# Gate-loop attention and SwiGLU feed-forward on one core: weights pieces no longer wait for rotated rows, and weights weigh half as much in the list schedule

## The chip, the cores and the metric

The kernel runs on one core of a Trainium2 chip. The metric is the device time of one execution in microseconds (us): the median of three runs, lower is better. The profile is a separate execution of the same program; times inside it count from the start of its span.

## The reference, cut to what matters

The first half is a linear attention with complex gates, the second a feed-forward network on its output.

```python
# 4 batches x 8 heads, 768 steps, head width 48
mag = np.sqrt(a_re * a_re + a_im * a_im)
scale = np.minimum(mag, 0.999) / (mag + 1e-06)
ar, ai = a_re * scale, a_im * scale                  # a complex gate for each step and feature
for t in range(S):
    new_re = ar[t] * S_re - ai[t] * S_im             # the state is turned and shrunk by the gate
    new_im = ar[t] * S_im + ai[t] * S_re
    S_re, S_im = new_re + outer(k[t], v[t]), new_im
    y[t] = q[t] @ S_re
# x: (3072 tokens, 384 features), w_gate and w_val: (384, 1536), w_out: (1536, 384)
xn = x / np.sqrt(np.mean(x * x, -1) + 1e-06) * rms_g
out = (silu(xn @ w_gate) * (xn @ w_val)) @ w_out
```

The three weight matrices come as 64-bit floats, so the kernel narrows them itself.

## The kernel before, in words

**Chunks, units, groups.** The 24 chunks n of 128 tokens are handled one after another. Gates are prepared by units u: unit 0 is chunk 0, unit 1 is chunk 1, and from unit 2 on a unit is two chunks. The feed-forward runs by groups g of two chunks.

**Gates of a unit** (`gates(u)`). ScalarE and VectorE compute the size of the gates (squares, reciprocal roots, a running product by scans), then their angle (Arctan, running sum by scans, then Abs and two Sin), and VectorE multiplies q and k with cosine and sine into a tile `rot`. Six DMAs issued by SyncE (`kq<-rot`, line 1123) then carry the rotated rows of a chunk from `rot` into the layout `kq` that the attention reads; their landing is what the attention waits for. `kq` and `rot` exist twice, for even and odd chunks.

**Attention of a chunk** (`attend(n)`). TensorE computes scores (`bank<-kq`, two halves in two PSUM banks), VectorE copies them under the causal mask into `am` (two copies), TensorE computes y (`bank<-am,ve` and `bank<-kq,state`), transposes k (`bank<-ident,kq`, evacuated by ScalarE as `kt`) and updates the state (`bank<-vn,kt`; VectorE adds and decays it as `state`). Then the norm: ScalarE squares y (`sq`), TensorE sums it (`bank<-ones,sq`), VectorE makes `ssv` of it, GpSimd its power of -1/2 (`rs`), TensorE spreads that over the partitions (`bank<-ident,rs`), and VectorE writes the normed rows `xT`.

**Feed-forward of a group** (`feed(g, xT)`). Six blocks b; each is six matmuls with `wg` into one bank and six with `wv` into another (the trace shows two passes for each, so x12), ScalarE takes Silu of the first (`sg`), VectorE the product (`hT`). The product with `wo` follows in parts of four matmuls (x8), some of which stand between the blocks.

**Weights.** Twelve pieces: pieces 0 to 5 are `wg` and `wv` in thirds (even pieces `wg`, odd `wv`, 1.5 MB each), pieces 6 to 11 are sixths of `w_out` (768 KB each). GpSimd issues the DMA of a piece (`fetch`) into a place inside `wo` or `hT` that an earlier piece has left, and a copy of one element into `junk`, which waits for the landing. A piece also waits until the piece two before it has landed. Narrowing a piece (`narrow`) is one conversion on ScalarE and three operations on VectorE: a shift (`TENSOR_SCALAR`), a mask (`SCALAR_TENSOR_TENSOR`) and an addition (`CUSTOM_DVE_ANT_0` in the trace). Piece 4 has one more wait: `CLEAR = {4: 1}` lets it wait for `cleared[1]`, a one-column copy by GpSimd (`seen<-kq`) that itself waits for the rotated rows of chunk 1. The same copy is made for chunk 0.

**What sets the order.** Nothing is ordered by hand. Every operation is recorded with an estimated duration and its dependences (`add`). `dates` gives it a due time, back from its users, and shifts that by the entry of its stage in the table `flow.shift`; stages are for example ("w", 4), ("kq", 2), ("attend", 1). `schedule` then walks through time, takes on each free engine the ready operation with the earliest due time, and models the transfers: each issuing queue has its first DMA in flight, and the flying ones share the DMA engines in proportion to their `packet`. The order that results is fixed in the program: at run time every engine works strictly through its list. Where the scheduler expects TensorE to stand still before 62 us, it puts in idle matmuls (`bank<-rot`, "fillers") that keep TensorE's clock up. All operations are issued from line 676, so the profile is read by tiles.

Of the kernel before, what the change touches and what calls it, by code (L numbers as in the profile page):

```python
# [461 lines left out]
class Flow:  # L462
# [9 lines left out]
    turn = 0.0  # L472
# [50 lines left out]
    def add(self, eng, calls, dur, reads=(), writes=(), table=None, land=None, due=None, after=(), behind=(), late=None, mode=None, group=None):  # L523
        op = dict(i=len(self.ops), eng=eng, calls=calls, dur=dur, deps=set(), table=table, land=land,
                  base=due, late=late, mode=mode, group=group, stage=self.stage, behind={o["i"] for o in behind})
        self.ops.append(op)
        op["deps"].update(o["i"] for o in after)
        for ap in reads:
            self.note(op, ap, False)
        for ap in writes:  # L530
            self.note(op, ap, True)
        return op
# [146 lines left out]
def fast(tc, ctx, qT, kT, v, a_re, a_im, w_gate, w_val, w_out, rms_g, out, H, bad):  # L679
# [107 lines left out]
    def run(x):  # L787
        n = 1
        for step, size in reversed([tuple(y) for y in x.ap][0 if x.tensor.name in outside else 1:]):
            if step != n:  # L790
                break
            n *= size
        return n

    def dma(o, x, eng="SP", slow=0.0, **kw):
        n = mybir.dt.size(o.dtype)
        for s in o.shape:
            n *= s
        row = mybir.dt.size(o.dtype) * min(run(o), run(x))
        load = n / row * (0.006 + 50.3e-6 * row) / 16  # L800
        op = add(eng, [(QUEUE[eng].dma_start, (), dict(out=o, in_=x))], 0.85 if eng == "POOL" else 0.62, [x], [o],
                 land=2.0 + 1.4 * load + slow, **kw)
        op["slow"] = slow
        op["load"] = load
        op["packet"] = max(0.07, 0.006 + 50.3e-6 * row * (2 if eng == "POOL" and row == 2048 else 1))
        return op

    def mms(list_, dur, **kw):
# [53 lines left out]
    row = room("row", [P, C])  # L862
# [31 lines left out]
    for o, order in ((band, "p (x h) -> p x h"), (head, "p (x h) -> p h x")):  # L894
        add("DVE", [(nc.vector.tensor_reduce, (), dict(out=o, in_=ident.rearrange(order, h=H), axis=mybir.AxisListType.X,
                                                       op=ALU.add))], 0.3, [ident], [o], late=LATE)
# [22 lines left out]
    AHEAD = 2  # L919
    landed = {}  # L920

    CLEAR = {4: 1}

    def fetch(i, piece, raw, eng):
        to, ap, c, f = piece
# [7 lines left out]
        else:  # L933
            wait = []
        if eng == "POOL" and i in CLEAR:
            wait = wait + [cleared[CLEAR[i]]]
        sent = dma(raw3, src, eng, after=wait)
# [48 lines left out]
    turn = {}  # L986
# [59 lines left out]
    def gates(u):  # L1046
        ns = UNITS[u]
        nt = len(ns)
        T = nt * C
        t = loaded.pop(u) if u in loaded else load_kq(u, load_gates(u))  # L1050
        flow.stage = "size", u
        re, im, q, k = (t[x] for x in ("re", "im", "q", "k"))
        t1, t2, t3, t4, t5 = (t[f"t{i}"] for i in range(1, 6))
        act(t1, re, AF.Square)
        act(t2, im, AF.Square)
        if u in SUMMED:
            sums = []
            for i in range(nt):
                cs = slice(i * C, (i + 1) * C)
                ps = bank()[:, 0:ND * C].rearrange("p (j t) -> p j t", j=ND)  # L1060
                mms([(ps, ident, x[:, :, cs], a == 0, a == 1) for a, x in enumerate((t1, t2))],
                    2 * mm_time(ND * C))
                sums.append(ps)
                act(t2[:, :, cs], ps, AF.Abs_reciprocal_sqrt)
        else:
            tt(t1, t1, t2, ALU.add)
            act(t2, t1, AF.Abs_reciprocal_sqrt)
        act(t2, t2, AF.Square, scale=-EPS_MAG, bias=ones)
        act(t3, re, AF.Abs_reciprocal_sqrt, due=-200.0 if u == 0 else None)
        act(t3, t3, AF.Square, due=-200.0 if u == 0 else None)  # L1070
        if u in SUMMED:
            for i in range(nt):
                cs = slice(i * C, (i + 1) * C)
                ts(t1[:, :, cs], sums[i], CAP * CAP, None, ALU.min)
        else:
            ts(t1, t1, CAP * CAP, None, ALU.min)
        for j in range(ND):
            for i in range(nt):
                cs = slice(i * C, (i + 1) * C)
                scan(t4[:, j, cs], t2[:, j, cs], t1[:, j, cs], 1.0, ALU.mult, ALU.mult)  # L1080

        tt(t["f"], t["in"], t3.unsqueeze(1).to_broadcast([P, 2, ND, T]))
        stt(im, t5, 2.0, t3, ALU.subtract, rev=True)
        act(re, re, AF.Abs, bias=mid)
        act(re, re, AF.Relu, bias=width, accum=range_[:, u:u + 1])

        flow.stage = "root", u
        root = act(t2, t4, AF.Abs_reciprocal_sqrt)
        act(t1, t2, AF.Square)
        stt(t1, t1, -0.5, t4, ALU.mult)  # L1090
        stt(t2, t1, 1.5, t2, ALU.add)
        tt(q, q, t4)

        roots.append(root)
        yield
        flow.stage = "turn", u
        act(im, im, AF.Arctan, after=roots[-2:])
        last = turn.get(u - 1) if ns[0] % NCH else None
        for j in range(ND):
            scan(t3[:, j], im[:, j], zeros[:, 0:T], last[:, j] if last is not None else 0.0,  # L1100
                 ALU.add, ALU.add)
        n = t5.bitcast(I32)
        act(n, t3, AF.Copy, scale=0.5 / PI)
        stt(im, n, -2 * PI, t3, ALU.mult, ALU.add)
        turn[u] = im[:, :, T - 1:T]
        act(t5, im, AF.Abs)
        act(t3, im, AF.Sin)
        act(t5, t5, AF.Sin, scale=-1.0, bias=halfpi)

        for i, n_ in enumerate(ns):  # L1110
            e = slice(i * C + C - 1, i * C + C)
            tt(ends[:, :, n_:n_ + 1], t4[:, :, e], t2[:, :, e])
        flow.stage = "rot", u
        tt(t["f"], t["f"], t2.unsqueeze(1).to_broadcast([P, 2, ND, T]))
        for i, n_ in enumerate(ns):
            cs = slice(i * C, (i + 1) * C)
            for a, f in enumerate((t5, t3)):
                x = tt(rots[n_ % 2][:, a * ND:(a + 1) * ND].rearrange("p j (o t) -> p j o t", t=C), t["kq"][:, :, :, cs],
                   f[:, :, cs].unsqueeze(2).to_broadcast([P, ND, 2, C]))
                if not started:  # L1120
                    started.append(x)
        for n_ in ns:
            moved[n_] = [dma(kqs[n_ % 2][r:D2:2 * ND], rots[n_ % 2][:, r], "SP") for r in range(2 * ND)]
            if n_ < 2:
                cleared[n_] = copy(seen, kqs[n_ % 2][:, 0, 0:1], eng="POOL")
                cleared[n_]["dur"] = 1.2
        send_decays(u)
# [5 lines left out]
    def bank():  # L1133
        i = bank_turn[0]
        bank_turn[0] = (i + 1) % 4
        return banks[i]
# [231 lines left out]
    for in_, limit, op in ((ef, P_MIN, ALU.is_ge), (ef, 1.0, ALU.is_le), (range_, 0.0, ALU.is_le),  # L1368
# [15 lines left out]
    flow.warm = dict(after=started, until=WARM, call=[  # L1384
        (nc.tensor.matmul, (banks[3][:, 0:C],), dict(lhsT=filler[:, 0:C], rhs=filler[:, C:2 * C], start=True, stop=True))])
    flow.shift = {
        ("attend", 0): -38.4, ("attend", 1): -1.9, ("attend", 2): -16.2, ("attend", 3): -0.7,
        ("attend", 4): -35.7, ("attend", 6): -12.2, ("attend", 11): -3.9, ("attend", 18): 6.0,
        ("attend", 19): -5.7, ("attend", 20): -1.5, ("attend", 21): 11.1, ("attend", 22): 4.2, ("feed", 4): 7.5,
        ("feed", 7): 1.6, ("feed", 8): 4.4, ("feed", 9): 16.9, ("feed", 11): -26.3, ("kq", 2): -10.9,  # L1390
        ("kq", 6): -3.3, ("kq", 7): -15.8, ("kq", 9): 8.6, ("load", 1): -4.5, ("load", 2): -33.3,
        ("load", 3): 50.7, ("load", 11): -5.2, ("load", 12): -6.8, ("norm", 0): -0.8, ("norm", 1): -5.1,
        ("norm", 5): -4.6, ("norm", 16): 4.4, ("norm", 20): 1.8, ("norm", 21): -20.2, ("norm", 22): -8.0,
        ("root", 1): -1.3, ("root", 2): -5.7, ("root", 3): 41.8, ("root", 5): 2.8, ("root", 9): 9.4,
        ("rot", 1): -4.3, ("rot", 2): 0.4, ("rot", 3): -2.6, ("rot", 5): 10.3, ("rot", 10): -10.2,
        ("rot", 12): 4.7, ("size", 2): -2.7, ("size", 3): 14.9, ("size", 7): -0.3, ("size", 10): 14.6,
        ("size", 11): 53.4, ("size", 12): 18.6, ("state", 0): 20.7, ("state", 1): -6.7, ("state", 2): -18.1,
        ("state", 3): -5.4, ("state", 4): -2.1, ("state", 10): 0.2, ("state", 14): -4.9, ("state", 20): -17.7,
        ("turn", 0): -5.1, ("turn", 1): -18.8, ("turn", 4): 7.1, ("turn", 5): 47.3, ("turn", 6): -2.5,
        ("turn", 8): -28.6, ("turn", 9): 0.3, ("turn", 11): -2.5, ("w", 0): -2.6, ("w", 3): -20.3, ("w", 5): -3.8,  # L1400
        ("w", 6): -7.5, ("w", 10): -31.1, ("y", 0): -12.7, ("y", 1): -1.0, ("y", 7): 1.7, ("y", 10): 4.5,
        ("y", 11): -0.4, ("y", 15): 0.8, ("y", 17): -2.8, ("y", 20): 2.2,
    }
    flow.schedule()
    with tc.manual_schedule():
# [51 lines left out]
```

## Time and profile before

| | us |
|---|---|
| median of 3 runs (lowest, highest) | 721.65 (721.41, 721.87) |
| the profiled execution, whole | 723.45 |
| its span, first to last instruction | 721.7 |
| TensorE busy | 685.9 (95%) |
| VectorE busy | 476.2 (66%) |
| ScalarE busy | 328.6 (46%) |
| GpSimd busy | 65.5 (9%) |
| mean granted TensorE clock | 0.991 |

The span is 1.75 us shorter than the profiled execution's own time and equal to the median of the runs to 0.05 us. A share of busy time is an average: here the stretch up to about 118 us, where the gates of the first chunks, the weights and the first group meet, is very different from the 600 us that follow.

### The profile page before, as it was taken

What the parts mean: (1) busy time and instruction counts of PE and PEld (TensorE: products, weight loads), DVE (VectorE), ACT (ScalarE), POOL (GpSimd) and SP (SyncE); (2) the same over time, 40 slices, a digit from 0 to 9 for tenths busy, and PEclk for the clock granted to TensorE, in tenths of its full rate; (3) what the DMA queues carried; (4) which work ended last, traced back from release to release, by engine and by line L of the source; (5) the groups of instructions that cost most, each with busy time, mean ns of one, the idle gap of its engine ahead of it and who ended that gap; (6) DMA issues with size and microseconds to landing.
All of it is one profiled execution on the core that took longest, in us unless ns stands there. A gap on an engine that the chain in (4) does not pass through costs nothing.

```text
span 721.7 us, 16275 instructions
## 1 busy us (share of the span) xinstructions
PE 685.9 (95%) x6910; PEld 602.1 (83%) x6910; DVE 476.2 (66%) x756; ACT 328.6 (46%) x448; POOL 65.5 (9%) x106
## 2 busy tenths in 40 slices
PE   0779999999999999999999999999999999999996
PEld 0768877886889889889889889889889889989886
DVE  8998879878788778768757677777553432224121
ACT  8657648866677663837324743735510110010010
POOL 3232100010100001110001001010010000000000
PEclk9988999999999999999999999999999999999999
DMA  9897555535566355463554445444132410020000
GB/s 305 257 279 218 167 147 142 139 97 129 172 151 150 63 131 137 117 173 75 162 111 116 134 106 154 123 90 96 29 75 41 107 7 5 22 56 2 23 1 27
DMA packets 104000, 81.83 MB, mean 113 GB/s; under 512 B 41936, under 2 KB 94416, under 8 KB 103920
## 3 DMA queue, kind: packets, MB, share of 16 engines
q1 hardware_dynamic: 98560, 64.78, 32.8%
q0 software_dynamic: 4416, 15.35, 9.4%
q8 instruction: 56, 0.92, 0.6%
q10 hardware_dynamic: 944, 0.59, 0.3%
q14 instruction: 24, 0.20, 0.1%
HBM read 55.84 MB, written 4.72 MB: 84 GB/s over the span
## 4 chain that ended last, share of the span: by engine, by line
PE 86%; DMA 4%; DVE 4%; ACT 3%; SPq 1%; issue 1%; POOL 0%; DVEq 0%; ACTq 0%; POOLq 0%
PE bank L676 86%; DMA wo<-in_w_val_dram 2%; DMA wo<-in_w_gate_dram 1%; SPq L676 1%; DVE turns L676 1%; ACT turns L676 1%; ACT t L676 1%; ACT L676 1%; DMA in<-in_a_re_dram 1%; DVE rot L676 1%; DVE wv L676 1%; DMA decay<-ends 0%; DVE hT L676 0%; ACT wo L676 0%; POOL rs L676 0%
## 5 line engine op out<-in xcount | busy, mean ns | idle before, releaser
L676 PE MATMUL bank<-xT,wg 128*128 128x256 f32 x864 | 203.5, 386 | 0.0
L676 PE MATMUL bank<-xT,wv 128*128 128x256 f32 x864 | 201.4, 383 | 0.0
L676 PEld LDWEIGHTS bank<-xT,wg 128*128 128x128 f32 x864 | 162.7, 192 | 23.7 <-issue 2.0
L676 PEld LDWEIGHTS bank<-xT,wv 128*128 128x128 f32 x864 | 161.2, 190 | 22.2 <-issue 0.8
L676 ACT ACTIVATE sg<-bank 128x512 f32<-128x512 f32 x72 | 43.0, 597 | 171.1 <-PE bank L676 170.8
L676 DVE TENSOR_TENSOR hT<-bank,sg 128x512 f32<-128x512 f32 x72 | 49.6, 689 | 104.6 <-PE bank L676 99.1
L676 PE MATMUL bank<-wo,hT 128*128 128x192 f32 (+1 forms) x576 | 117.2, 356 | 0.6 <-DVE hT L676 0.5
L676 PEld LDWEIGHTS bank<-wo,hT 128*128 128x128 f32 x576 | 96.0, 190 | 12.3 <-DVE hT L676 1.0
L676 ACT ACT_TABLE_LOAD x64 | 82.1, 1283 | 17.7 <-DVE rot L676 10.2
L676 POOL TENSOR_TENSOR rs<-ssv,mhalf 128x1 f32<-128x1 f32 x24 | 24.8, 1034 | 501.2 <-DVE ssv L676 455.2
L676 DVE TENSOR_TENSOR rot<-kin,turns 128x768 f32<-128x768 f32 x48 | 44.1, 952 | 5.1 <-DMA kq<-rot 4.8
L676 ACT ACTIVATE kt<-bank 128x384 f32<-128x384 f32 x40 | 19.4, 488 | 57.8 <-PE bank L676 55.9
L676 PE MATMUL bank<-sums,hT 128*128 128x192 f32 x240 | 44.3, 327 | 0.0
L676 DVE COPY_PREDICATED am<-causal,bank 128x512 f32<-128x512 int32 x48 | 33.6, 725 | 15.3 <-PE bank L676 15.2
L676 PEld LDWEIGHTS bank<-sums,hT 128*128 128x128 f32 x240 | 39.8, 190 | 0.2
L676 DVE TENSOR_TENSOR hT<-hT 128x768 f32<-128x768 f32 x40 | 38.2, 956 | 0.7
L676 PEld LDWEIGHTS bank<-kq 96*32 96x32 f32 x1536 | 31.0, 112 | 8.8 <-issue 7.6
L676 PE MATMUL bank<-am,ve 128*32 128x128 f32 x768 | 37.3, 275 | 0.0
L676 PE MATMUL bank<-kq 96*32 96x128 f32 (+3 forms) x1536 | 35.4, 240 | 1.1 <-DMA kq<-rot 1.1
L676 ACT ACTIVATE t<-t 128x768 f32<-128x768 f32 (+1 forms) x39 | 30.7, 789 | 8.7 <-DVE t L676 8.3
L676 ACT ACTIVATE turns<-in 128x768 f32<-128x768 f32 (+1 forms) x39 | 30.1, 790 | 8.1 <-DVE in L676 6.1
L676 PE MATMUL bank<-kq,state 96*32 96x128 f32 x640 | 32.5, 272 | 0.2 <-DVE state L676 0.2
(123 smaller groups left out, 727.7 us busy)
## 6 DMA issues: line engine op xcount, KB each, us to landing
kq<-rot SPq DMA_DIRECT2D x144, 128.0 KB, 3.1
kin<-in_q_dram SPq DMA_DIRECT2D x24, 192.0 KB, 3.4
kin<-in_k_dram SPq DMA_DIRECT2D x24, 192.0 KB, 3.5
wo<-in_w_gate_dram SPq DMA_DIRECT2D x6, 768.0 KB, 5.9
wo<-in_w_val_dram SPq DMA_DIRECT2D x6, 768.0 KB, 5.7
wo<-in_w_out_dram SPq DMA_DIRECT2D x6, 768.0 KB, 4.6
out_dram<-ot SPq DMA_DIRECT2D x23, 192.0 KB, 2.3
in<-in_a_re_dram SPq DMA_DIRECT2D x11, 384.0 KB, 4.3
```

Source lines behind the costliest of these rows:

```text
L676: fn(*args, **kw)
```

## The change

Four things change in the code. Piece 4 no longer waits for chunk 1's rotated rows (`CLEAR` is empty). The two GpSimd copies `seen<-kq` are not made. In the scheduler's model of transfers, a piece of weights with rows over 2048 bytes has its `load` times 0.78 and its `packet` times 0.5. And the table of shifts is another one: many entries are changed and some are new.

```diff
-        load = n / row * (0.006 + 50.3e-6 * row) / 16
+        piece = eng == "POOL" and row > 2048
+        load = n / row * (0.006 + 50.3e-6 * row) / 16 * (0.78 if piece else 1.0)
...
-        op["packet"] = max(0.07, 0.006 + 50.3e-6 * row * (2 if eng == "POOL" and row == 2048 else 1))
+        op["packet"] = max(0.07, 0.006 + 50.3e-6 * row * (0.5 if piece else 1.0))
...
-    CLEAR = {4: 1}
+    CLEAR = {}
...
-            if n_ < 2:
+            if n_ in CLEAR.values():
                 cleared[n_] = copy(seen, kqs[n_ % 2][:, 0, 0:1], eng="POOL")
                 cleared[n_]["dur"] = 1.2
...
     flow.shift = {
-        ("attend", 0): -38.4, ("attend", 1): -1.9, ("attend", 2): -16.2, ("attend", 3): -0.7,
...
+        ("attend", 0): -38.4, ("attend", 1): -1.9, ("attend", 2): -4.4, ("attend", 3): -1.4, ("attend", 4): -35.7,
...
+        ("load", 0): 14.7, ("load", 1): -4.5, ("load", 2): -50.1, ("load", 3): 105.5, ("load", 5): 38.7,
...
+        ("turn", 12): -31.4, ("w", 0): -3.6, ("w", 1): -1.4, ("w", 2): -15.6, ("w", 3): -22.6, ("w", 4): -1.7,
...
```

The arithmetic is the same; what the program gets is another order on each engine. Up to the second group the orders of the two built programs differ in these places:

- GpSimd: the two `seen` copies are gone; `rs` of chunk 0 now stands before the `junk` copy that waits for piece 5, then come that copy and the DMA of piece 4, then the DMA of piece 7, then `rs` of chunk 1.
- ScalarE: of the first angles, the conversion of piece 1 no longer stands between the rounding copy and Abs of unit 0. Later, the conversion of piece 5 comes after the squares and roots of unit 2 instead of before them, still ahead of `sq` of chunk 1. In group 0 the operations on `in` with `mid` and `width` and the first square of unit 3 come after the Silu of block 2, ahead of unit 2's Arctan.
- VectorE: the masked copies `am` of chunk 0 come before the addition of piece 1 and before all operations on piece 0. The addition for piece 5 and the first sum of unit 2 come after `xT` of chunk 1 instead of before it. Piece 4's three operations come after the scans of unit 2 and after the first `hT`.
- TensorE: 33 fillers before the first group's matmuls instead of 46; 16 instead of 33 before the scores of chunk 0. The first half of chunk 1's scores stands before chunk 0's state update, the second half after it. Chunk 1's state update stands before the first group's matmuls instead of between blocks 4 and 5. Before the scores of chunk 2 there is one part of the product with `wo` instead of two.
- SyncE: the first look at `w_gate` (a second load of the weights, `wo<-in_w_gate_dram`, used by a range test) stood between the rotated rows of chunks 2 and 3 and now comes after the six `decay` loads and the values of chunk 5; the q and k loads of unit 3 now precede the six `decay` loads.

## The prediction

> **What bounds the kernel now.** I read the page first, for shares and slices, then the chain of waits in order of time, then the timelines of the engines up to 120 us.
>
> ```profile
> span 721.7 us, 16275 instructions
> ...
> PE 685.9 (95%) x6910; PEld 602.1 (83%) x6910; DVE 476.2 (66%) x756; ACT 328.6 (46%) x448; POOL 65.5 (9%) x106
> ...
> PE   0779999999999999999999999999999999999996
> ...
> PEclk9988999999999999999999999999999999999999
> ```
>
> TensorE is busy in all slices but the first three and the last. Of its 35.8 us of idle time, 19.8 lie before its first instruction and 6.1 after its last. The chain of waits says the same: from 108.85 us it is matmuls.
>
> ```profile
> 90.65 9.07 DMA wo<-in_w_gate_dram
> ...
> 102.52 3.37 DMA decay<-ends
> ...
> 108.85 444.69 PE bank L676 x4007
> ```
>
> So the order after that is worth little (its gaps sum to 0.75 us), and the change is priced by when TensorE gets through the start. Three marks carry it: F, the first matmul of group 0; K, the scores of chunk 2; G, the first matmul of group 1. TensorE's timeline:
>
> ```profile
> 55.81 4.89 PE L676 MATMUL bank<-xT,wg 128*128 128x256 f32 x12
> 60.54 2.75 PE L676 MATMUL bank<-xT,wv 128*128 128x256 f32 x12
> ...
> 92.62 2.74 PE L676 MATMUL bank<-wo,hT 128*128 128x384 f32 x8
> 96.41 1.33 PE L676 MATMUL bank<-kq 96*32 96x128 f32 x64 [1.05 <-DMA kq<-rot]
> ...
> 118.23 2.78 PE L676 MATMUL bank<-xT,wg 128*128 128x256 f32 x12
> ```
>
> F is 55.81, K 96.41, G 118.23. Start to start, a block of twelve passes takes 2.59 us, but the first takes 4.73: the clock was halved. Windows of ten us (last columns: granted clock, DMA share, GB/s):
>
> ```profile
> 50.00:60.00 10.00, 7.66 (x30) 6.66 (x31) 9.17 (x9) 6.26 (x10) 4.49 (x5) 0.66 0.78 243
> ...
> 90.00:100.00 10.00, 8.95 (x146) 7.02 (x148) 7.42 (x13) 4.67 (x6) 0.42 (x1) 1.00 0.72 204
> ```
>
> **The removed wait and the copies: nothing.** GpSimd's timeline:
>
> ```profile
> 32.98 0.78 POOL L676 DMA_DIRECT2D wo<-in_w_val_dram  x1 [10.73 <-DVE wv L676]
> ...
> 43.65 1.44 POOL L676 COPY seen<-kq 96x1 f32<-96x1 f32 x1
> 45.03 0.80 POOL L676 DMA_DIRECT2D wo<-in_w_gate_dram  x1
> ```
>
> Piece 5 goes out at 32.98, when VectorE has added piece 1; piece 4 at 45.03, behind the copy. In the new order piece 4's DMA stands behind the `junk` copy that waits for piece 5. Piece 5 itself leaves later, since the masked copies of chunk 0 now precede the addition of piece 1 (about 34.6, below). It took 10.9 us (32.98 to 43.88, when ScalarE converts it), so piece 4 leaves at about 45.6: the wait for rows is replaced by one for piece 5 of the same length. The copies' 0.17 and 1.44 us lay in GpSimd's idle time. Piece 4's narrowing (0.87 + 1.68 + 1.67 on VectorE) ends at about F + 12.7, and block 4 reads it at F + 20.8: hidden by blocks 0 to 3.
>
> **Up to F: 2.8 us earlier.** On ScalarE the conversion (1.57 us) that delayed Abs of unit 0 is gone from that place, and VectorE can write `rot` about 1.3 us sooner. Little of it arrives: SyncE stood idle to 29.87 before chunk 1's row loads though `rot` was ready at 28.1, so its own queue held it. But the last row load no longer meets piece 5. In two short stretches of SyncE (29.8 to 30.4, and 33 to 33.7, when piece 5 had just gone out) rows took:
>
> ```profile
> DMA to landing us min/median/max: 2.4/2.4/2.4
> ...
> DMA to landing us min/median/max: 2.4/3.7/5.0
> ```
>
> Now they go out by 32.9 at the latest and piece 5 at 34.6: landed by 35.3, where it was 38.1 (33.1 + 5.0). If they meet again, 38.1 stays. From 35.3: first half of the scores 0.66 and state update 0.86 (TensorE, 36.8); then VectorE has twelve operations up to `ssv` of chunk 1: state 0.5, additions of pieces 3, 0, 2 at 1.67 each, masks 1.68 twice, shifts 0.87 twice, `am` 1.28, `xT` 0.5, two small 0.2, together 12.6: 49.4. GpSimd's power took 1.31 and 2.01 (take 1.7), the spread 0.6, a filler and hand-overs 0.7, `xT` 0.55: F at about 53.0 instead of 55.8. ScalarE (roots of unit 2, conversion of piece 5 from 45.5, `sq`) is ready by 48 to 50, not later. Chunk 1's state update (0.9 us) is now done before F. I expect the clock halved at F as before (fewer fillers): 2.6 us lost of 1.7 to 3.4, against 2.15.
>
> **From F to K: the gain goes.** Before, unit 2's Arctan ran at 73.01, F + 17.2. Now it stands behind the Silu of block 2, which needs TensorE at F + 2.6 + 5 x 2.59 = F + 15.6; then ScalarE has Silu 0.5, a conversion 0.75, a square 0.75, `mid` 0.83, `width` 1.05, a table load 1.28 and Arctan 0.77: F + 21.5. VectorE's scans take 1.95, the rounding copy and a table load with two Silu keep ScalarE to F + 25.35, then 0.87 on VectorE, Abs and two Sin 2.4 on ScalarE: F + 29.1. VectorE meanwhile does states and two additions to 29.4, then turns 1.7 and the first `rot` 0.9: F + 32.0 = 85.0. It was:
>
> ```profile
> 85.14 1.83 DVE L676 TENSOR_TENSOR rot<-kin,turns 128x768 f32<-128x768 f32 x2
> ```
>
> The first of these two ended at 86.1: F + 30.3. So F's 2.8 us have shrunk to 1.1. From there to the landing it was 10.3 us (86.1 to 96.4), not the 6.3 of undisturbed rows (3.9 to issue six, 2.4), because pieces 10 and 11 went out just ahead:
>
> ```profile
> 81.70 0.72 POOL L676 DMA_DIRECT2D hT<-in_w_out_dram  x1 [7.09 <-DVE wo L676]
> 82.84 0.72 POOL L676 DMA_DIRECT2D hT<-in_w_out_dram  x1 [0.41 <-DVE state L676]
> ```
>
> The same pieces wait for the same additions now and go out at F + 28 and F + 28.9, 81 to 82: as close ahead as before. The look at `w_gate`, now later, was issued behind these rows on the same queue; I give nothing for it. K at 85.0 + 10.3 = 95.3. TensorE gets there with one `wo` part fewer and no state update: thirteen blocks, F + 2.6 + 33.8 = 89.4. It stands still for 5.9 us instead of 1.05, and the second `wo` part is still to do.
>
> **From K to G.** Before 21.8 us, of which 0.54 idle; now 21.3 + 2.6 = 23.9. VectorE has 18 us of work for group 1 in that time and the `decay` values land near 106, as before; TensorE hides both. To this comes the clock. In the trace, gaps of 0.94 and 1.64 us with fillers between them (49.8 to 53.9) were enough to halve it, and the first block lost 2.15 us; the single gap of 1.05 at 95.4 was not (1.00 in the window of 90 to 100). [...] By the trace's rows it is sure, at about 2.2. I take the rows; the ends are 0 and 3.4.
>
> **Sum.** G = 95.3 + 23.9 + 2.2 = 121.4 against 118.23: 3.2 us later. On the profiled span, 721.7 becomes 724.9 (own time 723.45, 726.6). The median of the runs equals the span, so 721.65 becomes 724.8.
>
> **Rivals.**
> *Faster: the rows of chunk 2 come in time.* One mechanism: pieces 10 and 11 have drained when the rows go out, or Arctan is not held up. Then K is F + 36.4 (no stall) to F + 39[...], and G = 53.0 + 36.4 + 23.9 = 113.3 to 115.9, which is 2.3 to 4.9 us earlier: 716.7 to 719.3. It decides from K = 92.9 on, where G is 1.4 earlier. For it: VectorE's own work from `xT` to the first `rot` is only 29.1 us. Against it: Silu of block 2 before Arctan in ScalarE's list, and 10.3 us of landing.
> *No change: the stall comes, the clock stays.* G = 95.3 + 23.9 = 119.2, 1.0 later: 722.6.
> *Slower still: chunk 1's rows meet piece 5 again,* since nothing keeps weights from them. Landed at 38.1, F is 55.8 and all after it 2.8 later: 727.6.
> That the removed wait does nothing by itself is part of my own case; then the order alone decides.
>
> **How the numbers follow.** A measurement of this kernel can tell about 0.2%, 1.4 us. My case has 0.50, with its own range of 723 to 726.6 (F and the landing each by 1 us, the clock from 0 to 3.4), nearly all of it slower. The faster rival has 0.25, no change 0.15, slower still 0.10. Faster 0.25, same 0.16, slower 0.59. The range of 8 in 10 goes from 718.5 (half of the faster rival) to 727.0.
>
> **What would show it.** Right: piece 4 issued within 1 us of 45; F at 52 to 54.5; Arctan of unit 2 later than F + 20; TensorE idle 4 to 7 us before the scores of chunk 2, with DMA kq<-rot as the releaser; a clock under 1.00 in the window of 90 to 100. Wrong: that idle time under 2 us, or F before 51. If G is early and the time is not, my reading of the last 600 us was wrong.

## The result, and the profile after

The changed kernel takes 729.64 us (median of 15 runs, 724.6 to 734.77); the kernel before, on the same chips, 723.07 us (721.41 to 725.64). The ratio is 1.0088, 95% interval 1.0063 to 1.0114: slower by 0.9% (6.6 us between the medians). The prediction had the sign, but half the size (3.2 us), and 729.64 lies over its range, 718.5 to 727.0. What is new is the spread: 10 us from run to run, where before has 4 here and up to 6 beside the later runs.

The first profile of the changed kernel fell on one of its short runs (725.26 us):

```profile
span 723.6 us, 16211 instructions
...
PE 683.5 (94%) x6884; PEld 599.4 (83%) x6884; DVE 475.7 (66%) x756; ACT 333.2 (46%) x451; POOL 71.4 (10%) x104
```

TensorE's timeline of it, with the scores of chunk 0, then F, K and G, then the scores of chunk 6 (in brackets: idle time just before, and what ended it):

```profile
31.57 2.36 PE L676 MATMUL bank<-kq 96*32 96x128 f32 x64 [2.56 <-DMA kq<-rot]
...
56.48 2.86 PE L676 MATMUL bank<-xT,wg 128*128 128x256 f32 x12 [0.71 <-DVE xT L676]
...
94.08 1.33 PE L676 MATMUL bank<-kq 96*32 96x128 f32 x64 [3.10 <-DMA kq<-rot]
...
117.75 2.78 PE L676 MATMUL bank<-xT,wg 128*128 128x256 f32 x12
...
170.86 1.33 PE L676 MATMUL bank<-kq 96*32 96x128 f32 x64 [1.27 <-DMA kq<-rot]
```

The stall before the scores of chunk 2 has grown from 1.05 to 3.10 us, as foretold, yet G is 0.5 us *earlier* than before. The time is lost after G: 1.27 us before the scores of chunk 6 (in before's order they stand behind more parts of the `wo` product and wait for nothing), 0.57 us at 324.7. Part of this loss lies in the profile of before, which is short after G (603.5 us; three more profiles of its order have 604.3 to 604.9). And a short run alone would tell a wrong story: the second profile below is of a long one.

### The profile page after: what moved, and what is told of

It reads as the page before. It is cut to its first block, busy times and chain, and to the rows that moved or that the text cites. A ratio compares the mean times of both kernels' runs of the same rounds, so it can differ in the third digit from the quotient of the medians.

```text
span 723.6 us, 16211 instructions
## 1 busy us (share of the span) xinstructions
PE 683.5 (94%) x6884; PEld 599.4 (83%) x6884; DVE 475.7 (66%) x756; ACT 333.2 (46%) x451; POOL 71.4 (10%) x104
## 4 chain that ended last, share of the span: by engine, by line
PE 84%; DMA 5%; DVE 4%; SPq 3%; ACT 2%; issue 1%; DVEq 0%; ACTq 0%
PE bank L676 84%; SPq L676 3%; DMA kq<-rot 2%; DMA ve<-in_v_dram 1%; DVE turns L676 1%; ACT t L676 1%; DVE wo L676 1%; DMA in<-in_a_im_dram 1%; DMA in<-in_a_re_dram 1%; DVE hT L676 1%; ACT turns L676 0%; DVE rot L676 0%; ACT L676 0%; DVE in L676 0%; DVE t L676 0%
## 5 line engine op out<-in xcount | busy, mean ns | idle before, releaser
L676 PE MATMUL bank<-xT,wg 128*128 128x256 f32 x864 | 201.1, 382 | 0.7 <-DVE xT L676 0.7
L676 PEld LDWEIGHTS bank<-xT,wg 128*128 128x128 f32 x864 | 161.0, 190 | 23.7 <-issue 1.8
L676 PEld LDWEIGHTS bank<-kq 96*32 96x32 f32 x1536 | 31.6, 113 | 14.3 <-issue 12.7
L676 PE MATMUL bank<-kq 96*32 96x96 f32 (+3 forms) x1536 | 36.2, 241 | 6.9 <-DMA kq<-rot 6.9
L676 PEld LDWEIGHTS bank<-sums,hT 128*128 128x128 f32 x240 | 39.8, 190 | 0.3
L676 DVE TENSOR_TENSOR hT<-hT 128x768 f32<-128x768 f32 x40 | 38.2, 956 | 0.8
L676 PE MATMUL bank<-rot 128*128 128x128 f32 x66 | 13.5, 368 | 21.6 <-DVE rot L676 21.6
```

What stands on the lines that cost most here:

```text
L676: fn(*args, **kw)
```

## The experiments

Each kernel was timed beside before, whose median was then 722.7 to 723.0 us. The ratio is to that, with its 95% interval. "Gap" is TensorE standing still. A "short" run of the changed kernel takes 724 to 726 us, a "long" one 728 and more.

**The same kernel again.** No edit.

> The changed kernel once more, nothing edited, so that a second profile of it is there. Its median was 729.64 us, with runs from 724.6 to 734.8 us, while its one profile (725.26 us) was among its shortest. Theory A (the new order puts scores on TensorE before their rotated rows have landed: 3.10 us of standing still at 90.98 us and 1.27 us at 169.59 us in that profile, and in a longer run these last longer): the gaps of TensorE before scores with releaser kq<-rot add up to over 5 us in a longer run, and the time lost against the first profile lies before 200 us. Theory B (the gaps are as long, but in a longer run the granted clock is halved after one of them, which loses 2 to 4 us each time): the gaps stay within 1 us of 3.10 and 1.27 us and a stretch of half clock stands behind 90 or 170 us. Theory C (what varies is later, in loads of x and v): gaps with releasers other than kq<-rot, after 200 us. Time: median 727 to 732 us.

Median 729.9 us (8 runs, 725.45 to 733.93), ratio 1.0087 (1.0055 to 1.012). This profile is of a long run (732.05 us, span 730.3). TensorE:

```profile
34.33 2.36 PE L676 MATMUL bank<-kq 96*32 96x128 f32 x64 [3.83 <-DMA kq<-rot]
...
59.38 2.93 PE L676 MATMUL bank<-xT,wg 128*128 128x256 f32 x6 [0.29 <-DVE xT L676]
...
99.24 2.36 PE L676 MATMUL bank<-kq 96*32 96x128 f32 x64 [3.32 <-DMA kq<-rot]
...
102.23 4.14 PE L676 MATMUL bank<-wo,hT 128*128 128x384 f32 x8
...
125.61 2.78 PE L676 MATMUL bank<-xT,wg 128*128 128x256 f32 x12
```

G is 7.9 us later than in the short run, and the two spans differ by 6.7. So the long run is made before G, in three places. F is 2.9 us later; the scores of chunk 0 began 2.8 us later. The first block of group 0 then runs at half clock (4.97 us from start to start, 2.69 in the short run; granted clock 0.51 from 57.28 to 64.10 us), which is the 2.3 us between the two in F to K. And behind K, for another 2.7 us, the same 64 score matmuls take 2.36 instead of 1.33 us, the `wo` part 4.14 instead of 2.77: half clock. The window of 98 to 105 us (last three columns: granted clock, DMA share, GB/s), first of the short run, then of the long:

```profile
98.00:105.00 7.00, 7.00 (x193) 5.98 (x192) 5.98 (x11) 3.43 (x7) 0.81 (x1) 1.00 0.48 107
```

```profile
98.00:105.00 7.00, 5.76 (x73) 4.46 (x74) 5.64 (x10) 3.93 (x5) 0.00 (x0) 0.51 0.73 203
```

Behind the gap of 3.32 us the clock was halved for 6.8 us (0.51 in this window), behind the one of 3.10 us it was full (1.00). Theory B holds. A's sign (gaps of over 5 us) does not tell the two apart: they sum to 7.9 us here, and to 6.9 in the short run. C does not hold: in all twelve profiles of this kernel, with and without the additions below, the stretch from G to the end takes 604.7 to 606.3 us, while G lies anywhere from 116.4 to 125.6.

**The wait alone.** Before's order to the letter; only the two copies do nothing.

```diff
+    for op in flow.ops:
+        if op in cleared.values():
+            op["calls"] = []
```

> The kernel before in its own order, with the calls of GpSimd's two copies (seen <- kq) emptied: the wait of piece 4 for the rotated rows of chunk 1 goes, nothing moves. If the wait and the copies are worth nothing by themselves (my step 1), the time is that of before within 0.2% and piece 4 is issued within 1 us of 45.0 us. If the missing wait is what costs (weights pieces meet the rotated rows again): slower by 2 us or more, with the rows of chunk 1 landing later than 41 us and a gap of TensorE before the scores of chunk 1 of over 2.5 us.

722.2 us (14 runs), ratio 0.9992 (0.9976 to 1.0009). Piece 4 goes out 0.8 us sooner than before (GpSimd's timeline):

```profile
44.25 0.80 POOL L676 DMA_DIRECT2D wo<-in_w_gate_dram  x1
```

The wait and the copies are worth nothing; no collision took their place.

**Which part makes the order bad?** Four kernels, each with a part of the change and a list made anew: the code of after with the old table; the wait taken out, nothing else; the weights halved (the two lines of the change), nothing else; the new table, nothing else.

```diff
# the wait taken out, nothing else
-    CLEAR = {4: 1}
+    CLEAR = {}
...
-            if n_ < 2:
+            if n_ in CLEAR.values():
```

> The change of the code (no wait, no copies, half the packet and 0.78 of the load for a weights piece) with the table of shifts of before. If the table was made for the new costs and carries nothing else, theory A expects a loss here too, wherever scores are placed ahead of their rows: the gaps before scores in this order tell how much, 0.2 to 1.5% slower than before. If only the new table carries the loss: within 0.2% of before. The rival that a shift table fits one cost model alone expects this to be slower than the changed kernel itself (over 731 us).

> The kernel before with its own table and its own weights in the list schedule; only the rule that piece 4 waits for the rows of chunk 1 and the two copies are taken out, and the list is made anew. So the order moves by this part alone: on VectorE the masked copies of chunk 1 stand behind three more operations on weights. If the halved weights carry the loss (they move the masked copies of chunk 0 ahead of work on VectorE that could be done before the rows land), this stays within 0.6% of before (723 to 727 us), and TensorE's gap before the scores of chunk 0 is absent, since the fillers there stay. If any new order is as bad with a table that was not made for it (the rival), it costs as much as the whole change, 729 to 731 us.

> The kernel before with only the weights changed in the list schedule (half the packet, 0.78 of the load); its table, the wait and the copies stay. VectorE's order is that of the run with the whole code change and the old table (729.78 us), TensorE's but for one filler; GpSimd now stands before piece 5 until the rows of chunk 1 are in. If the weights carry the loss and the wait nothing: 728 to 731 us, with TensorE idle 2 to 4 us before the scores of chunk 0. If rows colliding with weights pieces are what costs (theory C), this is back within 0.3% of before (721 to 725 us).

> The kernel before (its wait, copies and weights) with the table of shifts of after: the fourth corner beside before (722.7 us), new code with the old table (729.8 us) and the changed kernel (729.6 us). If a table fits only the costs it was found with, this is slower than before by 0.8% or more (over 728 us). If the new table is the better one and the new costs spoil it: 719 to 723 us.

| weights, wait in the list | table of before | table of after |
|---|---|---|
| both as before | 1 (before) | 732.28 us, 1.0134 (1.0114 to 1.0154) |
| wait gone only | 732.66 us, 1.0149 (1.0123 to 1.0174) | - |
| weights halved only | 727.63 us, 1.0069 (1.0047 to 1.0092) | - |
| both as after | 729.78 us, 1.0092 (1.0064 to 1.0119) | 729.64 us, 1.0088 (1.0063 to 1.0114) |

Every list made anew is slower than before's by 0.7 to 1.5%, whichever part made it; so in the main the rival of these expectations won, though not to the letter: it had the old table with the new code over 731 us, and that one is as slow as the changed kernel, within theory A's 0.2 to 1.5%. That the halved weights carry the loss alone is refuted by the wait taken out, which is worse still: F there at 61.7 us. The new table with the old weights has F at 65.8. The new table brings the new code nothing (729.64 against 729.78). That a table fits only the costs it was found with is one reading of this; that before's list is simply a good one, and most others are not, is another, and no run tells them apart. Nor are the new lists slow in every run: one of eleven with the old table took 721.35 us, one of twelve with the halved weights 722.01.

**One `wo` part moved.** The changed kernel, its second `wo` part of group 0 put ahead of the scores of chunk 2, as in before.

```diff
+        part = next(op for op in wos if op["order"] > first["order"])
+        pe.remove(part)
+        pe.insert(pe.index(first), part)
```

> The changed kernel with one TensorE group moved: the second part of the output product of group 0 stands ahead of the scores of chunk 2, where it does in the kernel before. Theory A: the gap of 3.10 us before those scores goes to under 1.2 us and the median falls by 2 to 4 us (to 726 to 728 us). Theory B: it falls by more, 4 us or over, because the gap that halves the clock in longer runs is gone, and the spread of the runs shrinks to under 5 us. If the gap at K was paid back anyway by the work of group 0 that has to be done before group 1 (rival): within 0.2% of the changed kernel.

728.47 us (7 runs), ratio 1.0068 (1.0039 to 1.0096): 1.2 us under the changed kernel, with intervals that overlap, as the rival had it. TensorE shows why:

```profile
95.49 2.93 PE L676 MATMUL bank<-wo,hT 128*128 128x384 f32 x4 [2.48 <-DVE wo L676]
98.35 1.48 PE L676 MATMUL bank<-kq 96*32 96x128 f32 x64
```

One stall takes the place of the other: half of the part waits 2.48 us for VectorE to narrow its weights. In the list it stands behind the scores, where that wait is hidden.

**Idle matmuls ahead of K.** The changed kernel, with nine matmuls of the identity in front of the scores of chunk 2, into the bank which these scores then overwrite (the edit shortened).

```diff
+    scores[0]["calls"] = [(nc.tensor.matmul, (banks[4][:, 0:C],),
+        dict(lhsT=ident, rhs=ident, start=True, stop=True))] * 9 + scores[0]["calls"]
```

> The changed kernel with nine idle matmuls (of the identity matrix, 0.27 us each at full clock by the fillers of the start, 2.5 us together) ahead of the scores of chunk 2. Work that the product needs stays where it is; the first score comes no sooner. If the clock after the gap at K is what makes the long runs (theory B; 6.8 us at half clock behind a gap of 3.32 us cost 3.4 us in the second profile): the median falls by 2 to 3.5 us (to 726.5 to 728 us), the granted clock is 1.0 from 94 to 110 us, and G - K stays under 24 us. If the lateness of the start decides and the clock is small change: within 1 us of the changed kernel.

726.64 us (11 runs), ratio 1.0057 (1.0035 to 1.0078). By chance its profile (span 729.5) has the same start as the second one of the changed kernel, F 59.49 and K 99.48:

```profile
95.95 2.17 PE L676 MATMUL bank<-ident 128*128 128x128 f32 x18
99.48 1.33 PE L676 MATMUL bank<-kq 96*32 96x128 f32 x64 [1.36 <-DMA kq<-rot]
...
123.20 2.78 PE L676 MATMUL bank<-xT,wg 128*128 128x256 f32 x12
```

K to G takes 23.7 us at full clock (1.00 from 90 to 110 us) where it took 26.4: the half clock behind K costs 2.7 us there. Not all of it arrives: the span is only 0.8 us shorter, since this profile takes 606.3 us from G on, with 1.32 us before the scores of chunk 6. The median moved by 3, but the two intervals overlap, and two kernels below that hold the same nine matmuls are at 728 and 729 us again. So the pair of profiles is the evidence, and a gain in the median is not shown.

**Masked copies later.** In the changed kernel, two weight operations of VectorE go ahead of the masked copies of chunk 0. VectorE's order by tiles, not code:

```diff
 wv<-hT,wv
+wv<-wo,wv   (addition of piece 1)
+wg<-wo      (shift of piece 0)
 am<-causal,bank x2
-wv<-wo,wv
-wg<-wo
 state<-bank,decay
```

> The changed kernel with two operations of VectorE (the addition of piece 0 and a shift of the next piece, 1.7 and 0.9 us) put ahead of the masked copies of chunk 0. In the changed kernel VectorE stood idle 1.54 + 0.34 us (first profile) and 3.29 + 0.34 us (second) for those copies, because the scores wait for rows that land at 31.5 to 34.3 us. Theory D (VectorE's idle time there is what makes F late): the idle time before the masked copies goes under 1 us, the sum of squares of chunk 1 and F come 1 to 2.5 us sooner, and the median falls by 1 to 3 us. If F hangs on rows, loads of v and GpSimd alone: F stays at 56 to 60 us and the median within 1 us of the changed kernel; a masked copy that is now behind its scores would make F later.

(The addition is piece 1's: odd pieces are `wv`.) 728.47 us (6 runs), ratio 1.0093 (1.0071 to 1.0114), and F at 58.6: no gain, theory D falls. VectorE's idle time did go, and came back three operations on:

```profile
35.39 0.73 DVE L676 COPY_PREDICATED am<-causal,bank 128x512 f32<-128x512 int32 x1 [0.89 <-PE bank L676]
...
42.38 0.55 DVE L676 TENSOR_TENSOR state<-bank,decay 96x384 f32<-96x384 f32 x1 [5.20 <-PE bank L676]
```

From the scores of chunk 0 (34.01 us here) to this state update it is TensorE's own chain, at half clock (the 64 score matmuls take 2.37 us), that takes 8.4 us.

**Idle matmuls at the start.** To the nine ahead of K come ten ahead of the scores of chunk 0; in the second kernel also 15 more in TensorE's other gaps up to F (8, 1, 4 and 2).

```diff
+    flow.fillers += [(142.5, 10)]                                         # first kernel
+    flow.fillers += [(142.5, 10), (185.5, 8), (211.5, 1), (228.5, 4), (233.5, 2)]   # second
```

> The changed kernel with the nine idle matmuls ahead of the scores of chunk 2 (which alone gave 726.64 us) and ten more of the start's fillers (2.7 us at full clock) ahead of the scores of chunk 0, where TensorE stood still 2.56 to 4.5 us before rows landed and then ran 6.8 to 10.2 us at half clock. Theory: F is the landing of those rows plus 25 us; at full clock the two score blocks, the transposes and the value product are 1.5 to 2 us shorter of that: F at 54.5 to 57.5 us, median 724.5 to 725.5 us. If VectorE's and GpSimd's work from there to F covers TensorE's (rival): F stays at landing plus 25 us and the median within 0.7 us of 726.6 us.

> As the last one, with 8 fillers more ahead of the first rs transpose (where TensorE stood 2.6 us), 1 ahead of the sums of chunk 1, 4 ahead of the second rs, 2 ahead of F: the clock is granted in full from 30 to 110 us. Beyond the last one, the first block of group 0 takes 2.9 instead of up to 5 us: 1 to 2.5 us, median 722.5 to 724.5 us. If then the time is still over that of before (722.7 us), what is left is the start's own lateness (rows of chunk 0) and the standing still before chunks 2 and 6, not the clock.

728.08 us (6 runs), ratio 1.0063 (1.0042 to 1.0083), and 728.79 us (6 runs), 1.008 (1.005 to 1.011). No further gain, and neither expectation of the first holds whole: F came at 55.8 us, 23.3 us after the scores of chunk 0 began (24.9 and 25.1 without the ten), as its theory had it, but the median is over both forecasts. Its profile loses the time at K, where a gap of 3.40 us stands behind the nine idle matmuls and K to G takes 26.3 us, its start at half clock (the 64 score matmuls take 2.37 us). In the second, runs of 729 us had a mean granted clock of 0.994 to 0.995, higher than the 0.991 of the changed kernel's short run, so not the start's clock lengthened them. The second's median is 4 us over its forecast; and in its profile the clock was not full from 30 us on, as expected, but halved from 34.9 to 38.3 us (the 32 matmuls of `am,ve` took 1.94 us, 1.08 in the first kernel). Five more profiles of it follow.

> The changed kernel with idle matmuls at all its early gaps, a second profile. If the start makes the long runs: in a run of 728 us or over, scores of chunk 0 begin after 34 us, F is after 58 us and G after 121 us, with span minus G within 1 us of 605. If chunk 2's rows do: F within 1 us of 57.5, K later than 97 us. If it is lost later: G under 120.5 us and span minus G over 607 us.

> The same kernel, a third profile, with the same three readings: start (F after 58 us), chunk 2's rows (K - F over 39.5 us), or later (span minus G over 607 us).

> The changed kernel with its early gaps filled, a fourth profile. A short run (724 to 726 us) shows again F at 57.5, K at 94.7 to 95.7, G at 118.4 to 119.4 us. In a long one (over 728 us): F after 58.5 us if the start makes it; K - F over 39.5 us if chunk 2's rows do; span minus G over 607 us if it is lost later.

> The same kernel, a fifth profile, with the same three readings: F after 58.5 us, K - F over 39.5 us, or span minus G over 607 us in a run of over 728 us.

> The same kernel, a sixth profile, with the same three readings: F after 58.5 us, K - F over 39.5 us, or span minus G over 607 us in a run of over 728 us.

| profile | time | F | K - F | gap before K | G | span - G |
|---|---|---|---|---|---|---|
| first | 726.07 | 57.5 | 38.2 | 1.67 | 119.4 | 604.9 |
| second | 725.42 | 57.4 | 37.3 | 0.80 | 118.4 | 605.1 |
| third | 725.63 | 57.5 | 37.5 | 1.00 | 118.6 | 605.1 |
| fourth | 731.62 | 57.3 | 39.8 | 3.26 | 124.0 | 605.7 |
| fifth | 725.44 | 56.5 | 38.0 | 1.52 | 118.2 | 605.3 |
| sixth | 723.63 | 55.5 | 37.2 | 0.73 | 116.4 | 605.4 |

The fourth is the long run. Its start is as good as the others'; by the expectations' signs (K - F over 39.5 us) it is chunk 2's rows. K is late, in spite of 2.2 us of idle matmuls in front of it. GpSimd, where the copy waits for piece 11, in the fourth and in the fifth:

```profile
95.39 0.17 POOL L676 COPY junk<-hT 1x1 int32<-1x1 int32 x1 [6.58 <-DMA hT<-in_w_out_dram]
```

```profile
90.83 0.17 POOL L676 COPY junk<-hT 1x1 int32<-1x1 int32 x1 [2.85 <-DMA hT<-in_w_out_dram]
```

And TensorE at K, again fourth and fifth:

```profile
97.07 2.36 PE L676 MATMUL bank<-kq 96*32 96x128 f32 x64 [3.26 <-DMA kq<-rot]
```

```profile
94.50 1.33 PE L676 MATMUL bank<-kq 96*32 96x128 f32 x64 [1.52 <-DMA kq<-rot]
```

In the fourth, piece 11 lands 4.6 us later and the rows beside it take up to 8.0 us to land (4.5 in the fifth): the gap passes what the fillers cover, the clock is halved from 97.1 to 103.9 us (0.58 in the window of 98 to 105), and K to G takes 26.9 us. Late rows at K thus cost twice, once by themselves and once by the clock (K to G 26.9 us against the fifth's 23.7), and with the start (F 56.5 or 59.4 us) they make the spread as far as the profiles show it. Why piece 11 is slow in one run and not in another is open.

**The same remedy in before's order.** 17 more fillers in the start's gaps; then the same with the two copies emptied.

```diff
+    flow.fillers += [(152.5, 6), (177.5, 2), (211.5, 3), (219.5, 6)]
```

> The kernel before, its order untouched, with 17 more of its start's idle matmuls in TensorE's gaps at 35.5, 41.7, 49.8 and 52.3 us (1.80, 0.71, 0.94 and 1.64 us). In its profile the clock was halved from 43.1 to 46.5 and 53.3 to 60.1 us; the last one cost the first block of group 0 2.15 us, which lies on the path. If those gaps halve it: no half clock between 43 and 60 us, F to G 2.2 us shorter, median 720 to 721 us (0.997 of before). If the clock is halved anyway, or the fillers get in the way of what they wait for: 722 to 724 us.

> The kernel before in its own order, with 17 more idle matmuls in the start's gaps (which gave 721.27 us, 0.9974 of before) and without the calls of the two copies, so that piece 4 doesn't wait for rows. If the wait is worth nothing: 720.5 to 722 us, equal to that run within 0.7 us. If the wait was hiding a collision that the gaps concealed: over 722.5 us.

721.27 us (12 runs), ratio 0.9974 (0.9961 to 0.9987), and 721.58 us (22 runs), 0.998 (0.9966 to 0.9993). The first, its clock row and TensorE:

```profile
PEclk9999999999999999999999999999999999999998
```

```profile
56.32 2.86 PE L676 MATMUL bank<-xT,wg 128*128 128x256 f32 x12
...
115.57 2.78 PE L676 MATMUL bank<-xT,wg 128*128 128x256 f32 x12
```

No half clock up to the last block; F to G is 59.3 us instead of 62.4: the full clock in the first block accounts for 2.15, the stall of 1.05 us at K that this profile lacks for the rest. That pair overstates the fillers: before's order without them, but with the copies emptied, has 59.8 us from F to G in its profile, where the half clock (53.5 to 57.0 us) fell mostly ahead of F. The gain is what the medians say, a quarter of a per cent, and it beats both kernels. And without the wait it is the same: step 1 again.

## Why the prediction was wrong

| | predicted | short run | long run |
|---|---|---|---|
| F | 53.0 | 56.5 | 59.4 |
| F to K | 42.3 | 37.6 | 39.9 |
| K to G | 26.1 | 23.7 | 26.4 |
| G | 121.4 | 117.75 | 125.6 |
| span - G | 603.5 | 605.8 | 604.7 |

**The wait and the copies: right,** by two kernels. The place of piece 4 in the new list was not: it goes out at 51.74 us, not 45.6, because piece 5 itself left at 36.94 (not 34.6), landed 11.3 us later, and GpSimd's one-element copy behind it then took 3.5 us. As foretold, that is hidden.

**"Up to F: 2.8 us earlier": wrong, and this is the step that failed.** F came 0.7 to 3.6 us later than in before's profile, 3.5 to 6.4 later than forecast. The step took its whole gain from chunk 1's rows, landed at 35.3 us instead of 38.1, as if F hung on them. Before's trace says that it did not: TensorE came to the scores of chunk 1 at 43.04 us, 5 us after those rows, without waiting, and the chain of waits to F runs through piece 5 instead. TensorE with the scores of chunks 0 and 1, then the chain:

```profile
33.70 1.33 PE L676 MATMUL bank<-kq 96*32 96x128 f32 x64
...
43.04 2.36 PE L676 MATMUL bank<-kq 96*32 96x128 f32 x64
```

```profile
32.98 10.88 DMA wo<-in_w_val_dram
```

The step also took the work of chunk 0 as done when chunk 1's rows land: "first half of the scores 0.66 and state update 0.86 (TensorE, 36.8)". But the scores of chunk 0 start only at 31.6 to 34.3 us, and the state update came at 39.3 to 41.7. TensorE was never waiting for chunk 1's rows, which were there at 36.8 and 37.0. From the update to F my 16.2 us were fair (17.2 and 17.7): VectorE's work up to `ssv` is 12.5 us against my 12.6, but VectorE also stands still for TensorE, 1.9 us in the short run and 1.0 in the long one. TensorE in turn had waited for GpSimd's power of chunk 0, which took 2.9 us here and 1.3 before, and in the short run for values of chunk 1, which SyncE had issued only at 39.17 us:

```profile
44.59 0.50 PE L676 MATMUL bank<-ident,rs 128*128 128x128 f32 x2 [2.60 <-POOL rs L676]
...
49.74 0.30 PE L676 MATMUL bank<-am,ve 128*32 128x128 f32 x2 [0.54 <-DMA ve<-in_v_dram]
```

What was overlooked besides is what holds chunk 0's rows. In the short run they are issued from 21.5 us on, 1.6 us sooner than before, and gain nothing: the first lands at 29.73 us (29.80 before), behind a piece of weights that lands at 29.57 (29.21 before). The short run's timeline of GpSimd, where the copy waits for piece 2, and then its answer for the tile `kq` on SyncE:

```profile
29.68 1.76 POOL L676 COPY junk<-hT 1x1 int32<-1x1 int32 x1 [7.62 <-DMA hT<-in_w_gate_dram]
```

```profile
L676 SPq DMA_DIRECT2D kq<-rot x6: 575/626/667, 21.5 to 24.9; - x6
...
DMA to landing us min/median/max: 6.4/7.2/8.2
```

The first row takes 8.2 us and lands as that piece does; before, it was at most 6.6 us from a later start. In the long run the piece lands at 31.3 and the first row, issued at 22.57, at 31.4. In before's list 33 fillers and three more weight operations filled that time, and the scores began 2.2 us after the last row was there (33.70 against 31.47): late rows had slack. The new list has 16, so TensorE stands still 2.6 to 3.8 us and then works chunk 0 at half clock (the 64 score matmuls take 2.36 us in both profiles, 1.33 before). That the piece holds the rows is read from the times of landing; no run moved the piece out of their way. And neither the masked copies moved nor the fillers put back brought the median down, so what the late rows cost in time is read from the profiles, not measured by taking them away. The rival "slower still" had F no earlier than before, at a chance of 0.10, but for chunk 1's rows.

**F to K: too long by 2.4 to 4.7 us,** which hid most of the first error. The first `rot` ends at F + 30.1 (F + 32.2 where the first block ran at half clock), against 32.0. The landing after it is 7.1 to 8.1 us in most profiles and 9.6 to 9.8 in two (first score less the end of the first `rot`, in eleven profiles of this order); my 10.3 was the long case. So was the stall of 5.9 us: it was 3.1 to 3.3 us in the two profiles of the changed kernel, and 5.4 to 5.6 in the two with the late landing, their 2.2 us of idle matmuls counted in. (One sum on the way is off: 25.35 + 0.87 + 2.4 is F + 28.6, not F + 29.1. Nothing hangs on it, as VectorE's own work, to F + 29.4, ends later.)

**K to G and the clock: right in the long runs,** 26.4 against 26.1. Both ends that I kept (0 and 3.4) nearly occur: 23.7 us with nothing lost, and up to 26.9 in a later kernel. (Before's profile has half clock from 43.05 to 46.46 and from 53.29 to 60.12 us, which can cost 1.7 and 3.4 us.) But "by the trace's rows it is sure" was said of a gap of 5.9 us, which no profile has: of those that came, 3.10 us was followed by full clock and 3.26, 3.32 and 3.40 us by half. Leaning on rows of before's trace, where gaps of 0.94 and 1.64 us stood ahead of half clock, was right in kind: in the kernel with the new code and the old table a gap of 1.98 us at 93.6 was followed by half clock from 97.1 to 100.5 (a `wo` part of 4.27 us instead of 2.77).

**The sum: three terms fell short.** With span - G of 605.3 (mean of the two profiles) and 1.7 us around the span, the median of 729.64 means a G of about 122.6, 1.2 over mine. The other 3.6 of the 4.8 us come from taking span - G as before's 603.5 (1.8: in part the new stall at chunk 6, in part because before's profile was low), and from setting the median equal to the profile's span (1.75), as it was over three runs; over fifteen, before's median is 1.4 us higher. Both made the range too low as a whole; in the sum, F too early by 3.5 to 6.4 us and F to K too long by 2.4 to 4.7 pull against each other, so that a G within 1.2 us of the median's is luck. "If G is early and the time is not, my reading of the last 600 us was wrong" came true in the short run, by 2.4 us.

## What to carry to other kernels

A list tuned by hand-found shifts can lose by any change of its costs, as in all four parts here: judge what the new list does, not what the edit says. Before pricing a transfer that lands sooner, look whether the engine that reads it waited for it at all. Before counting a gain in the start, ask of each transfer on the path which bulk transfer it lands behind; issuing it sooner may buy nothing (here 1.6 us at the issue were 0.07 us at the landing), and a list without slack for it can vary more from run to run, as here (10 us against 4). A profile is one run: where runs spread by over 1%, take a second profile before explaining the first, and look whether short gaps before a late transfer cost a clock as well (here 2.7 us from K to G).

## What the runs showed of the hardware

- The granted clock behind gaps of TensorE. Before's profile has half clock (0.50) from 43.05 to 46.46 and from 53.29 to 60.12 us, the short run's from 31.29 to 38.12 and from 44.94 to 48.35; between those stretches and from there to 700 us it is 1.00 in both. Work behind the gap at K, in order of the gap (us):

| profile | gap | 64 score matmuls | `wo` part after them |
|---|---|---|---|
| nine idle matmuls ahead of K | 1.36 | 1.33 | 2.77 |
| all gaps filled, fifth | 1.52 | 1.33 | 2.77 |
| all gaps filled, first | 1.67 | 1.33 | 2.77 |
| new code, old table | 1.98 | 1.33 | 4.27 |
| changed kernel, short run | 3.10 | 1.33 | 2.77 |
| all gaps filled, fourth | 3.26 | 2.36 | 4.70 |
| changed kernel, long run | 3.32 | 2.36 | 4.14 |
| ten ahead of chunk 0, nine ahead of K | 3.40 | 2.37 | 4.07 |

The length of the gap does not sort them: 1.98 us was followed by half clock, 3.10 us was not. No run shows why.

- The first of chunk 0's rows landed up to 0.6 us after piece 2 (1.5 MB) in three profiles. The row, issued at 23.16 us (before), 21.55 (short run) and 22.57 (long run), landed at 29.80, 29.73 and 31.4; the piece came at 29.21, 29.57 and 31.3. SyncE issued these six rows and two loads of `v`, then stood still, and issued chunk 1's first row at 29.87, 29.79 and 31.45 us. Of chunk 1's rows, with no piece in flight, the first three took 2.4 us before and the first four 2.2 to 2.4 in the short run; its last two took 4.1 and 3.8.
